# Batch 0 cut into two parts of 384 tokens, in an attention and two-layer kernel on one core

## The chip, the core and the metric

The kernel runs on one core of one Trainium2 chip. The metric is the device time of one execution in microseconds (us); less is better. The time of the kernel before is the median of three runs. A separate execution was recorded by the hardware profiler, and every engine name below is the profiler's: PE is TensorE, DVE is VectorE, ACT is ScalarE, POOL is GpSimd, SP is SyncE, which here only issues DMAs.

## The reference

Attention over 4 batches of 8 heads, 768 positions and 64 elements per head, and a two-layer network with a leaky activation behind it. Three heads (0, 2, 6) see all earlier positions; the other five see the first 4 positions (the sinks) and a window of 64.

```python
scores = scale * np.matmul(q, k.transpose(0, 1, 3, 2))
causal = rel >= 0                              # rel = query position - key position
stream_keep = causal & (is_sink | in_win)      # 4 sinks, window 64
mask = np.where(retr, causal, stream_keep)     # is_retrieval = [1,0,1,0,0,0,1,0]
a = softmax(np.where(mask, scores, -1e9))
x = np.matmul(a, v)                            # to (3072 tokens, 512)
h = x @ w_in                                   # w_in: 512 x 2048
g = np.maximum(h, 0.0) + alpha * np.minimum(h, 0.0)
out = g @ w_out                                # w_out: 2048 x 512, out in float32
```

## The kernel before

**Units of work.** A segment n (0 to 15) is one pair of heads of one batch: batch n // 4, pair n % 4 out of `PAIRS = [(2, 6), (1, 5), (0, 4), (3, 7)]`. So segment 0 holds two full ("retrieval") heads, segments 1 and 3 two windowed ("stream") heads, segment 2 one of each. The keys of a head lie in an array of 128 rows of which 64 belong to that head and the others are zero (`kTs`), so that a score matmul can contract over 128 rows without taking anything from the other head.

**Names in ORDER.** The program is a list of items, `ORDER`, and is issued in exactly that order; each engine works through its own instructions in that order, and so does each DMA queue. An item's name is a letter, a segment, and mostly a head (0 or 1) and a part:

- `Lq`, `Lk`, `Lv` load rows from HBM (issued by SP; a few by ACT and POOL). `Cq`, `Ck`, `Cv` cast them to bf16; for batch 0 to 1 nearly all of these run on POOL. `Cv3.1` is on DVE and includes a copy of the sink rows.
- `Tq`, `Tk` transpose on PE, `tq`, `tk` copy the result out of PSUM. From segment 8 on, `Dq`, `Dk` do this by DMA.
- `S` are score matmuls into PSUM, `s` the exp on ACT that takes them to the buffer of weights (`eR` for full heads, `eS` for stream heads), `m` a multiplication by a 0/1 mask on DVE. Some `m` items (m14.0.2 and its like) cover no masked tile and issue nothing.
- `A` is weights times V on PE, with a column of ones that yields the sum; `a` is its reciprocal and the product on DVE; `X`, `x` transpose the result into `xT`, by PE and a DVE copy, or by a DMA.
- `Pt.f` is the first layer for token part t and block f of 128 hidden columns, four matmuls over the four segments of the batch (for the first blocks of t = 0 split into three items, `P0.f.0` for segments 0 and 1, `.1` for 2, `.2` for 3); `p` is relu(-h) on ACT, `g` the product and sum on DVE. `Ot.s.u` is a quarter of the second layer for 128 tokens, `o` the copy on ACT and the DMA to `out`. `L0` to `L2` and `l0` to `l2` are the last 128 tokens, in three cuts.
- `wi0` to `wi7` and `wo0` to `wo3` load the weights of the two layers through POOL's DMA queue, 256 KB and 512 KB (as bf16). Block f of the first layer needs wi(2k) and wi(2k+1) with k = f // 4. `sz`, `so`, `ro`, `vz`, `kz`, `kfz`, `nz` are fills; `nms`, `nmr`, `ms`, `mr`, `nr`, `ns` make masks.

**Masks and 64-row form.** In batch 0 (n < 4) a mask is added on PE: after each score matmul a second one multiplies the identity with a tile of large negative numbers (lines 466 and 505). From segment 4 on the mask is the item `m`. There, too, score matmuls are collected in a list, `burst`, which is emitted when an item comes up that may not stand beside it (`beside_burst`). If both heads have at least `SPLIT = 576` columns in the list, their matmuls are issued alternately, each on its own 64 rows of the array (line 434), so that two run side by side. Otherwise they are issued one by one over 128 rows (line 427). In batch 0 the scores go out directly (line 417).

**Token parts.** Each batch has two token parts, 512 and 256. A PSUM bank holds 512 columns, so for the 256-token part two blocks f share a bank and one relu. There are eight PSUM banks, taken least recently used first out of a list of choices.

Of the kernel before, what the change touches and what calls it, by code (L numbers as in the profile page):

```python
# [38 lines left out]
O1.0.2 Lk11 s9.0.0 m8.0.3 O1.0.3 x7 P2.4 o1.0 m9.0.0 s8.1.2 S9.1.1 S9.0.1 m8.1.1 m8.1.5 p2.4 S9.1.2 S8.0.5 S9.1.0
m8.0.0 near0 m8.0.1 Lk13 s9.0.2 s8.0.5 s9.1.2 m8.0.4 P2.14 P2.2 s9.1.1 Cv8 s9.0.1 g2.4 m8.1.3 m8.1.4 A8.1 P3.10 P2.3  # L40
p2.2 P2.0 g2.2 Cq10 m8.0.5 a8.1 p2.14 g2.14 p2.0 m9.1.2 P2.1 g2.0 p2.3 P2.7 p2.7 p2.1 A8.0 P3.0 g2.3 P2.5 Ck11 g2.1
P2.9 p2.5 P2.6 g2.7 near2 g2.5 s9.1.0 p3.10 p3.0 p2.9 Cv9 g3.10 P2.8 Lq11 Dk11.1 g2.9 P3.8 m9.1.0 P2.10 p2.8 m9.1.1
Lk12 P3.4 g3.0 A9.1 near1 p2.6 g2.8 Lq13 P2.13 Cq11 P2.15 p2.13 Dk10.1 Dk10.0 Dq10 g2.6 p2.10 g2.13 p3.4 Lq12 P3.6
g2.10 P3.14 p2.15 a9.1 g2.15 P2.11 O2.0.0 P2.12 g3.4 O2.0.1 p2.11 p3.8 g2.11 Ck12 S10.0.1 S10.0.4 s10.0.1 g3.8 p3.14
O2.0.2 s10.0.4 Dk11.0 O2.1.0 Dq11 p2.12 a8.0 g3.14 S10.1.1 S10.0.0 p3.6 g2.12 m10.0.4 S10.1.0 S10.0.5 s10.1.0 s10.1.1
O2.1.1 Lv11 Cq12 O2.0.3 g3.6 S10.0.3 S11.0.0 m10.1.0 s10.0.5 s10.0.0 S11.1.2 S11.1.0 m9.0.2 S10.1.2 S10.0.2 s10.0.3
Cq13 O2.1.2 m10.0.0 s10.1.2 Lv10 Ck13 m9.0.1 m10.1.2 s11.1.2 m11.1.2 s11.1.0 Dk12.0 P3.2 s10.0.2 p3.2 A9.0 s11.0.0
O2.2.0 Dq12 S11.0.2 S11.1.1 m10.0.5 O2.1.3 S11.0.1 m10.0.3 Cv11 m11.0.0 m10.1.1 Dk13.1 m11.1.0 X8 m10.0.1 s11.1.1 Cv10
P3.12 p3.12 m11.1.1 a9.0 s11.0.1 O2.2.1 g3.2 A10.1 Dk13.0 o2.1 Dk12.1 g3.12 a10.1 Dq13 A10.0 A11.1 O2.2.2 m11.0.1 X9
o2.0 O2.3.0 O2.2.3 S12.1.5 S12.0.4 S12.0.2 a10.0 s11.0.2 S12.1.2 m11.0.2 a11.1 S12.0.1 s12.1.5 A11.0 Lq14 a11.0 X11  # L50
# [12 lines left out]
a15.1 A15.0 p5.0 a15.0 p5.4 O4.1.1 g5.8 O4.0.0 a14.0 m4.1.2 O4.2.0 g5.4 X15 P5.10 O4.1.2 O4.0.1 O4.2.1 m8.0.2 x15 X14
O4.0.2 P6.8 P6.6 O4.0.3 p5.10 g5.0 P6.1 O4.3.3 O4.2.2 g5.10 P6.7 p6.8 o4.0 p6.7 p6.6 P7.6 g6.7 g6.8 O4.2.3 P6.10
O4.1.3 P6.3 p6.10 o4.3 g6.10 P7.4 o4.2 O5.1.0 O5.1.1 P7.0 p6.1 g6.6 P6.2 g6.1 p6.3 O5.0.0 g6.3 o4.1 P6.13 p6.13 P7.14
g6.13 O5.0.1 p6.2 p7.0 P6.0 g6.2 O5.1.2 P6.5 g7.0 P6.11 p6.0 g6.0 O5.0.2 p6.11 O5.1.3 p7.4 p6.5 g6.11 P7.10 p7.14
m8.1.2 o5.1 g6.5 m12.1.2 P6.9 P6.4 g7.4 p6.9 g6.9 p6.4 O5.0.3 g7.14 P7.2 O6.1.0 P6.15 g6.4 p7.2 P7.12 p6.15 O6.1.1
O6.1.2 g7.2 o5.0 O6.0.0 g6.15 P6.14 P6.12 O6.0.1 p6.14 O7.0.0 O6.0.2 g6.14 p7.6 p7.12 p6.12 g6.12 g7.6 O6.3.0 O6.2.0
O6.2.1 O6.0.3 P7.8 O6.2.2 O6.1.3 g7.12 O6.3.1 p7.8 o6.1 p7.10 O6.3.2 O6.3.3 g7.8 O7.0.1 o6.3 g7.10 o6.0 L0 O6.2.3
O7.0.2 o6.2 O7.0.3 L1 l0 L2 o7.0 l1 l2  # L70
""".split()


@with_exitstack
def kernel(
    ctx: ExitStack,
    tc: tile.TileContext,
    q: bass.AP,
    k: bass.AP,
    v: bass.AP,  # L80
    is_retrieval: bass.AP,
# [24 lines left out]

    class Tiles:

        def __init__(self, starts, masked):
            self.QS, self.RM = starts, masked  # L110
            self.RO = [sum(S - x for x in starts[:j]) for j in range(6)]
            self.RTOT = sum(S - x for x in starts[:6])
# [13 lines left out]
    def tiles(n):  # L126
        return FULL if full(n) else NEAR if n >= LAY else FAR

# [68 lines left out]
    def heads(n):  # L197
        return PAIRS[n % 4]
# [670 lines left out]
```

## Time and profile before

| what | value |
|---|---|
| runs | 231.18, 230.71, 230.88 us; median 230.88 us |
| profiled execution, span from its first to its last instruction (the profile gives no other time of it) | 230.0 us |
| median of the runs less that span | 0.88 us |
| busy: PE, DVE, ACT, POOL | 221.2, 153.3, 139.1, 47.1 us |
| granted TensorE clock | 1.000 |
| read from and written to HBM | 27.55 MB, 6.29 MB |

Busy time is the time in which an instruction of the engine was in flight. Matmuls are pipelined, so a short matmul counts as long as its latency; the distance between the starts of matmuls that follow each other is a better price. The chain that ended last is followed back from the last instruction, at each step to what released it. The windows cut the span into stretches and give each engine's busy time in them. A row of a group reads: line, engine, operation, output and inputs with shapes, count, busy us and mean ns, then idle time ahead of it and what ended it.

### The profile page before, as it was taken

Reading aid. Unit: us, or ns where it says so; the run is one execution under the profiler, and the core shown is the slowest. Engines: PE = TensorE matmul, PEld = TensorE weight load, DVE = VectorE, ACT = ScalarE, POOL = GpSimd, SP = SyncE. Lnnn points to the kernel's source line nnn. Section 1 sums busy time; section 2 is a strip of 40 time slices with the busy share of each in tenths; the row PEclk is TensorE's granted clock in tenths of the full one; section 3 lists DMA queues with packets and bytes.
Section 4 is the critical chain, followed back from the end, with each engine's and each line's share of the span. In section 5 each row is a group of like instructions: output and inputs, shape, how many; then the busy total and the mean of one; then the engine's idle time right before and its main releaser. Section 6 shows DMA issues by size and latency. Waiting matters only on the chain.

```text
span 230.0 us, 5212 instructions
## 1 busy us (share of the span) xinstructions
PE 221.2 (96%) x1974; PEld 136.7 (59%) x2002; DVE 153.3 (67%) x396; ACT 139.1 (60%) x280; POOL 47.1 (20%) x96
## 2 busy tenths in 40 slices
PE   7989889999999999999999999999999999999994
PEld 7777857555566655565466445556854555554553
DVE  5688768997647866999997349979990345545110
ACT  6679647999968567554864874498422333623232
POOL 6658758000430643000002100010000020000000
PEclk9999999999999999999999999999999999999999
DMA  6979999999999999899979999893310130110033
GB/s 197 299 184 279 246 250 218 231 212 180 209 234 158 230 220 238 157 216 183 184 139 186 211 249 183 163 197 61 62 36 0 48 137 1 46 48 1 0 137 137
DMA packets 92448, 36.62 MB, mean 159 GB/s; under 512 B 79472, under 2 KB 90632, under 8 KB 92424
## 3 DMA queue, kind: packets, MB, share of 16 engines
q1 hardware_dynamic: 86168, 26.97, 59.7%
q0 software_dynamic: 5792, 8.93, 17.3%
q10 hardware_dynamic: 464, 0.40, 0.5%
q8 instruction: 15, 0.25, 0.5%
q14 instruction: 9, 0.07, 0.1%
HBM read 27.55 MB, written 6.29 MB: 147 GB/s over the span
## 4 chain that ended last, share of the span: by engine, by line
PE 85%; DMA 10%; SPq 1%; issue 1%; DVE 1%; POOL 0%; ACT 0%; DVEq 0%
PE P L605 36%; PE P L625 34%; PE P L560 6%; DMA vf<-in_v_dram 5%; DMA kf<-in_k_dram 4%; PE P L434 4%; PE P L644 2%; PE P L427 1%; PE P L585 1%; PE P L369 1%; SPq L247 1%; DVE vb L312 0%; SPq L224 0%; SPq L210 0%; DVE vb L349 0%
## 5 line engine op out<-in xcount | busy, mean ns | idle before, releaser
L617 DVE SCALAR_TENSOR_TENSOR g<-neg,oma,P 128x512 bf16<-128x512 f32 (+1 forms) x128 | 72.9, 610 | 39.7 <-ACT neg L610 38.6
L605 PE MATMUL P<-xT,w_in_b 128*128 128x256 bf16 (+1 forms) x503 | 89.5, 325 | 0.4
L610 ACT ACTIVATE neg<-P 128x512 f32<-128x512 f32 x96 | 54.3, 608 | 52.2 <-PE P L605 43.4
L625 PE MATMUL P<-w_out_b,g 128*128 128x512 bf16 x349 | 84.3, 379 | 1.5 <-issue 0.6
L605 PEld LDWEIGHTS <-w_in_b 128*128 128x128 bf16 x512 | 48.7, 98 | 32.4 <-DVE g L617 0.4
L625 PEld LDWEIGHTS <-g 128*128 128x128 bf16 x368 | 34.5, 98 | 36.8 <-issue 1.3
L473 ACT ACTIVATE eR<-P 128x448 bf16<-128x448 f32 (+6 forms) x63 | 36.6, 621 | 13.6 <-PE P L434 5.1
L635 POOL DMA_DIRECT2D out_dram<-ot x18 | 9.9, 553 | 117.5 <-ACT ot L631 117.5
L571 DVE TENSOR_TENSOR xn<-P,rcp 128x448 bf16<-128x448 f32 (+1 forms) x32 | 19.5, 608 | 1.1
L631 ACT COPY ot<-P 128x512 f32<-128x512 f32 x23 | 13.2, 594 | 11.0 <-PE P L625 8.6
L527 ACT ACTIVATE eS<-P 128x384 bf16<-128x384 f32 (+1 forms) x25 | 13.5, 570 | 3.4 <-PE P L505 2.6
L521 ACT ACTIVATE eS<-P 128x352 bf16<-128x352 f32 x30 | 13.8, 490 | 1.5 <-PE P L427 1.0
L560 PE MATMUL P<-vb,eS 128*128 128x65 bf16 x260 | 11.3, 193 | 1.5 <-DVE vb L312 0.8
L417 PE MATMUL P<-qT,kT 128*128 128x192 bf16 (+13 forms) x68 | 11.5, 251 | 1.1 <-ACT eR L473 0.6
L560 PEld LDWEIGHTS <-eS 128*128 128x128 bf16 x260 | 10.2, 97 | 3.5 <-issue 1.9
L570 DVE RECIPROCAL rcp<-P 128x7 f32<-128x7 f32 (+1 forms) x32 | 6.3, 197 | 7.2 <-PE P L560 6.9
L536 DVE TENSOR_TENSOR eS<-eS,ms_near 128x352 bf16<-128x352 bf16 x30 | 9.4, 336 | 2.3 <-ACT eS L521 2.2
L434 PE MATMUL P<-qT,kT 64*128 64x176 bf16 (+17 forms) x172 | 10.9, 250 | 0.0
L560 PEld LDWEIGHTS <-eR 128*128 128x128 bf16 x276 | 9.6, 97 | 1.5
L434 PEld LDWEIGHTS <-kT 64*128 64x128 bf16 x172 | 6.8, 94 | 6.0 <-issue 5.7
L560 PE MATMUL P<-vb,eR 128*128 128x65 bf16 x276 | 10.1, 193 | 0.0
L483 DVE TENSOR_TENSOR eR<-eR,mr_near 128x128 bf16<-128x128 bf16 (+5 forms) x36 | 6.9, 225 | 4.3 <-ACT eR L473 4.3
(104 smaller groups left out, 183.7 us busy)
## 6 DMA issues: line engine op xcount, KB each, us to landing
out_dram<-ot POOLq DMA_DIRECT2D x18, 256.0 KB, 3.7
vf<-in_v_dram SPq DMA_DIRECT2D x22, 192.0 KB
kf<-in_k_dram SPq DMA_DIRECT2D x21, 192.0 KB
qf<-in_q_dram SPq DMA_DIRECT2D x18, 192.0 KB
qf<-in_q_dram SPq DMA_DIRECT2D x7, 384.0 KB
w_in_b<-in_moe_w_in_dram POOLq DMA_DIRECT2D x8, 256.0 KB, 9.5
w_out_b<-in_moe_w_out_dram POOLq DMA_DIRECT2D x4, 512.0 KB, 13.6
kf<-in_k_dram SPq DMA_DIRECT2D x9, 196.0 KB
```

The costliest lines, as they stand in the source:

```text
L417: nc.tensor.matmul(to, keys, queries, start=True, stop=stop)
L434: nc.tensor.matmul(to, keys[own], queries[own], start=True, stop=True)
L473: nc.scalar.activation(ebuf[n, hh][:, lo:hi].rearrange("p (x c) -> p x c", x=len(parts)), P[:, got[0]:got[0] + len(parts), 0:(hi - lo) // ...
L521: nc.scalar.activation(slots, sc[:, 0:352].rearrange("p (s c) -> p s c", c=176), AF.Exp, scale=scale)
L527: nc.scalar.activation(slots, sc.rearrange("p x (s c) -> p x s c", c=192), AF.Exp, scale=scale)
L560: nc.tensor.matmul(pav[:, i, :], e[:, o:o + 128], vv[:, j, hh, 0:D + 1], start=(m == 0), stop=(m == len(terms) - 1))
L571: nc.vector.tensor_tensor(xn[n][:, 0:nt, D * hh:D * hh + D], pav[:, :, 0:D], rcp.to_broadcast([128, nt, D]), op=ALU.mult)
L605: nc.tensor.matmul(psg[:, w * i:w * (i + 1)], w_in_b[:, c, 128 * fb:128 * (fb + 1)], xT[:, c, o:o + w], start=(x == 0), stop=(x == 3))
L610: nc.scalar.activation(neg[t, f], bank(held["P", t, f][0]), AF.Relu, scale=-1.0)
L617: nc.vector.scalar_tensor_tensor(g_buf[t % 2][:, fb, 0:w], neg[t, f][:, c], oma[:, fb:fb + 1], bank(got[0])[:, c], op0=ALU.mult, op1=ALU.add)
L625: nc.tensor.matmul(bank(held["O", t, s][0]), g_buf[t % 2][:, f, 128 * s:128 * (s + 1)], w_out_b[:, f, :], start=(f == 0), stop=(f == 15))
L631: nc.scalar.copy(ot, bank(got[0]))
```

## The change

Segment 0 is cut at token 384 (`FIRST`): its weights for queries 0 to 383 come first in the buffer, scored as before by `S0.h.0` with masks added on PE; the columns of queries 384 to 767 are four parts `S0.h.1` to `S0.h.4` of 480 columns each, one bank each, handled like those of later batches: collected in `burst`, and masked by `m0.h.3` and `m0.h.4` on DVE. The second exp part of segment 3 (`S3.h.1`) is treated in the same way (`m3.h.1`). `A`, `a`, `X` and `x` of segments 0 and 3 are issued in two parts each (`PARTS`). Batch 0 has token parts of 384 and 384; one block f fills one bank, so both parts have 16 relus of 384 columns. Segment 2's full head and segment 3's heads get weight buffers of their own in the space of `w_out_b`, whose loads come later, and segment 0's result lies in spare space of `g_buf[1]`. The whole of `ORDER` is written anew, from the first load to the last copy.

```diff
-        def __init__(self, starts, masked):
+        def __init__(self, starts, masked, cuts=(S,), ends=None):
             self.QS, self.RM = starts, masked
...
+            self.SEG, self.AT, o = [], {}, 0
+            for lo, hi in zip((0,) + cuts, cuts):
+                for j in range(6):
+                    a = max(lo, starts[j])
+                    if a < hi:
+                        self.SEG.append((j, a, o, hi - a))
...
+    FIRST = Tiles([128 * i for i in range(6)], [128] * 6, (384, S), [0, 384, 768, 1248, 1728, 2208, 2688])
+    PARTS = {0: (0, 3, 6), 3: (0, 4, NT)}
...
+    late = w_out_b.rearrange("p f c -> p (f c)")
+    eR_x = late[:, 0:E_R]
+    eS_x = [late[:, 8192 - E_S * (i + 1):8192 - E_S * i] for i in range(2)]
...
+    ebuf, n_e = {(2, 0): eR_x, (3, 0): eS_x[0], (3, 1): eS_x[1]}, [0, 0]
...
+    def late(n, m):
+        return n >= 4 or n in (0, 3) and m > 0
+
     def score_bank(n, hh, m):
-        held["S", n, hh, m] = got = take(*(SC2 if n < 4 else ANY))
+        held["S", n, hh, m] = got = take(*(ANY if late(n, m) else LOW if n in (1, 2, 3) and m == 1 and not RETR[heads(n)[hh]] else SC2))
...
     def one_score(n, hh, m, to, keys, queries, stop=True):
-        if n < 4:
+        if not late(n, m):
             nc.tensor.matmul(to, keys, queries, start=True, stop=stop)
         else:
             burst.append((n, hh, m, to, keys, queries))
...
-    TOK = [(b * S + o, w) for b in range(B) for o, w in ((0, 512), (512, S - 512))]
+    TOK = [(b * S + o, w) for b in range(B) for o, w in (((0, 512), (512, S - 512)) if b else ((0, 384), (384, S - 384)))]
...
-                if n >= 4:
+                if n >= 4 or n == 0 and m > 2 or n == 3 and m:
                     item(f"m{n}.{hh}.{m}", M_retr if RETR[h] else M_stream, n, hh, m)
```

Of the new ORDER, the stretch from the first V loads to the first layer, and three places where a batch's first layer begins:

```diff
+rox S1.0.0 tq2 s1.0.0 S1.1.1 kfz1 Ck3.0 Ck3.1 Tk3 Lq0.1 S1.0.1 Lv1 Cq0.1 tk2.1 tk2.0 S2.1.0 tk3.0 tk3.1 Tk0.1 s1.1.1
+Cv1 wi1 Lv3 Cv3.0 s2.1.0 S2.1.1 s2.1.1 s1.0.1 tk0.1 S0.0.1 Tq0.1 S0.0.2 Lv0 S2.0.1 s2.0.1 one tq0.1 Cv0 Cv3.1 S3.0.0
+warm1 s3.0.0 s0.0.1 S0.1.0 A3.0.0 S0.1.1 s0.1.0 a3.0.0 s0.0.2 nr A0.0.0 a0.0.0 wi0 S3.1.0 A0.1.0 wi3 szx1 Lv2 Cv2 so1
+s3.1.0 S0.1.2 Lq4 Cq4 A1.1 a0.1.0 Lk5 s0.1.2 wi2 S0.1.3 S3.1.1 s0.1.3 A3.1.0 a1.1 S2.0.0 s3.1.1 s2.0.0 X0.0 sox1
+a3.1.0 wi7 x0.0 S2.0.2 Lk4 X3.0 x3.0 A2.1 a2.1 S3.0.1 s2.0.2 wi6 S0.1.4 s0.1.4 s3.0.1 Tq4 A1.0 Lq5 s0.1.1 m14.0.2
+m0.0.3 A2.0 m0.1.3 a1.0 m0.1.4 A0.0.1 X1 a2.0 A0.1.1 x1 X2 P0.0.0 a0.1.1 x2 P0.2.0 P0.1.0 P0.3.0 P0.3.1 m3.0.1 P0.2.1
+m3.1.1 a0.0.1 Ck5.1 P0.2.2 A3.1.1 tq4 A3.0.1 a3.0.1 P0.3.2 X0.1 P0.0.1 P0.0.2 P0.4.0 P0.1.1 Ck5.0 m12.0.2 Tk5 P0.1.2
...
+S7.0.0 s6.1.0 s7.1.2 Cv6 nz0 A4.1 O0.1.0 O0.1.1 Lv11 s6.0.3 m6.1.1 s7.1.0 s7.0.0 m6.1.0 m7.1.1 a4.1 A6.1 X4 m6.0.3
+m7.0.0 m7.0.2 m7.1.0 m7.1.2 A6.0 X5 A7.0 Lq8 a6.0 a6.1 Cq9 O1.1.2 A7.1 O0.1.2 O1.1.3 X6 a7.0 a7.1 X7 O0.1.3 x6 x5 x7
+P2.1 Lq11 p2.1 g2.1 Ck8 Lv9 Dk9.0 o0.1 P2.14 P3.10 P2.9 p2.9 p3.10 Lq10 P2.15 g3.10 p2.14 g2.14 Dk8.0 P2.12 P2.10
...
+m11.0.2 Dk13.0 m11.0.1 A10.0 a10.0 A10.1 a10.1 O2.0.1 A11.0 a11.0 O3.0.1 O2.0.2 O3.0.2 O3.0.3 O2.0.3 X10 o3.0 X11
+P4.11 o3.1 o2.0 Ck15 P4.9 P5.12 p5.12 p4.9 Lv15 Dq12 P4.5 P4.8 g4.9 p4.5 g4.5 Dk14.1 P4.12 g5.12 Cv13 Lv14 Dq15 p4.12
...
+s14.1.1 s14.1.2 m14.1.2 m14.0.0 m14.1.1 s14.0.2 X12 m14.1.0 A14.1 O5.1.2 a15.0 a15.1 m14.0.3 a14.1 A14.0 O4.1.3 X15
+O5.0.1 O5.0.2 O5.0.3 o5.0 a14.0 X14 x15 P6.1 p6.1 P6.3 p6.3 g6.3 g6.1 o4.1 P6.4 P7.0 p7.0 P7.2 O5.1.3 g7.0 P6.9 p6.4
```

In the order before, the corresponding stretch ahead of the first layer reads:

```
s2.0.2 s3.1.1 ... X1 a2.0 S3.0.1 x1 s3.0.1 kfz1 s3.0.0 Tk4 Cv3.1 wi3 wi6 X2 m6.0.2 Tq5
x2 A3.1 P0.2.0 Lq6 tk4.0 a3.1 A3.0 P0.3.0 Ck5.0 Lq4 tk4.1 a3.0 wi7 P0.0.0 wi5 ms P0.1.0 Al kfz2 X3 Ck5.1 P0.1.1 Tk5
```

## The prediction

> **What bounds the kernel now.** I read the page's busy shares first, then the chain that ended last in order of time, then windows cut where the chain changes its nature. The chain:
>
> ```profile
> PE 85%; DMA 10%; SPq 1%; issue 1%; DVE 1%; POOL 0%; ACT 0%; DVEq 0%
> ```
>
> In order of time it is a start-up led by loads, and from 30 us on TensorE work without a gap:
>
> ```profile
> 20.28 7.32 DMA vf<-in_v_dram
> ...
> 27.69 0.60 DVE vb L349
> ...
> 28.31 1.05 DVE vb L312
> ...
> 29.40 0.50 PE P L560 x11
> ...
> 30.71 1.29 PE P L605 x6
> ```
>
> The last V rows of batch 0 land at 27.69; VectorE casts them and copies the sinks; `A3.1` and the first layer follow. The windows:
>
> ```profile
> core 0: us, PE busy (x) PEld busy (x) DVE busy (x) ACT busy (x) POOL busy (x), PEclk, DMA share, GB/s
> 0.00:29.73 29.73, 25.70 (x384) 22.55 (x385) 22.13 (x57) 21.90 (x29) 20.50 (x44) 1.00 0.99 241
> 29.73:51.32 21.59, 21.43 (x167) 12.97 (x167) 17.97 (x42) 17.07 (x36) 7.39 (x12) 1.00 1.20 227
> ```
>
> Before 29.73 TensorE looks busy, but that is time in flight. To find its work I price matmuls by their spacing in the chain: 216.5 ns for 512 columns (0.86 us for 4), 109 for 256 (0.87 for 8), 56 for 128 (0.34 for 6), 30 for the 65 columns of AV (0.39 for 13); between these 0.421 ns per column. Summed over ORDER: 214.0 us in all, 20.9 ahead of the first P item (`P0.2.0` at 29.73), 193.1 from there. Those 193.1 took until 227.18, 197.45 us: 4.4 us lost in 197, 0.45 of them in the first 3.5 us. So an edit pays in two ways only: an earlier first P item, or fewer columns after it; and it costs by new waits after it. The last output's DMA ends the span 2.8 us after TensorE; the new tail issues the same cuts, so this stays. The profiled span is 230.0, the median of the runs 230.88; I add 0.88 to any span.
>
> **The change, part by part.**
>
> *64-row form.* `emit_burst` interleaves the two heads only if each has 576 columns in the burst. I walked the new ORDER through `beside_burst`: every burst of batch 0 holds one head alone (S0.0.4 | S0.0.3 | S0.0.1 | S0.0.2 | S0.1.1 | S0.1.2 | S0.1.3 with S3.1.1 | S3.0.1 | S0.1.4), because a T, A, non-late S or other item closes each. All fall back to the 128-row form, at the old price. All stand ahead of the first P item too. Gain: 0. (Pairing all would have saved 1920 + 384 columns x 0.421 ns = 0.97 us.)
>
> *Masks to VectorE.* TensorE loses 6 mask matmuls of n = 0 (128 columns, 56 ns) and 6 of n = 3 (192, 148, 44: 82, 64, 30 ns per head): 0.34 + 0.35 = 0.69 us, all in the start-up, where it idles. VectorE gains 6 x 0.225 (the `mr` form of L483 reads 244 ns, its mean 225) + 2 x 0.377 (L534) = 2.1 us.
>
> *Regrouped bursts of later batches:* 10 lone bursts become 7: 0.28 us less.
>
> Sum by the same prices: 213.1 us in all, 20.0 ahead of the first P item (now `P0.0.0`), 193.0 after it. The columns after it are unchanged, so everything turns on when it starts and what is lost behind it.
>
> *384-token parts.* Rows, with the mean ns of one behind the comma:
>
> ```profile
> L610 ACT ACTIVATE neg<-P 128x512 f32<-128x512 f32 x96 | 54.3, 608 | 52.2 <-PE P L605 43.4 <-issue 3.3 <-DVE xn L571 2.6
> L617 DVE SCALAR_TENSOR_TENSOR g<-neg,oma,P 128x512 bf16<-128x512 f32 x64 | 46.5, 744 | 33.1 <-ACT neg L610 32.5
> L617 DVE SCALAR_TENSOR_TENSOR g<-neg,oma,P 128x256 bf16<-128x256 f32 x64 | 27.6, 475 | 6.5 <-ACT neg L610 6.1
> L534 DVE TENSOR_TENSOR eS<-eS,ms 128x384 bf16<-128x384 bf16 x15 | 5.4, 377 | 1.0 <-ACT eS L527 1.0
> ```
>
> Batch 0 has 128 P matmuls as before; 384 columns come to 163 ns, 20.8 us either way. Relu rises from 24 x 0.608 to 32 instructions, each between 0.508 (the 384-column exp of L527) and 0.608; I take 0.508, the nearest shape: +1.7 us on ScalarE. Prelu: 32 of about 0.61 (between 0.475 and 0.744) against 16 x 0.744 + 16 x 0.475: no change. Back to back, an instruction of ScalarE or VectorE starts some 0.12 us before the one ahead has ended (three relus take 1.57 us). At such intervals I count, from `P0.4.0` to `O0.0.0`, ScalarE 15.4 and VectorE 12.9 us beside 17.7 of TensorE: hidden; uncovered the relus would cost 1.7.
>
> *When P0.0.0 can start.* It needs x0.0 and x1, behind a long VectorE queue. Loads of equal cumulated bytes land as before (0.79 MB at 5.5, 1.18 at 7.9, 2.36 at 11.2, 3.15 at 14.3, 4.72 at 21.3, from the casts that waited). VectorE is through tk0.0 and kz1 at 7.7. After that up to x1, at intervals of the trace: 5 split kT copies x 1.13, tk2.0 0.95, tk0.1 0.95, tq0.1 0.93, ms 0.75, some ten fills 1.75, Cv3.1 1.6, four half-size a items x 0.55, four whole ones x 0.77, 6 masks x 0.18, x0.0, x3.0, x1 together 1.1: 20.1 us, so 27.8; the waits that I find by hand (Tk3, A3.0.0) bring 28.4, and 0.5 for handoffs not seen gives 28.9. Bounds: 28.4 without them, 30.5 if VectorE stalls as long as in the same stretch of before (2 us). Gain 29.73 - 28.9 = 0.8, and 0.1 of work.
>
> *Weights of the first layer.* They move behind work on the POOL queue: wi1 behind Cv1; wi0 and wi3 behind Cv0 and `nr` (1.25 us, which ran far behind all weights before); wi2 behind Cv2 and Cq4, which wait for Lv2 and Lq4. Before: issued 18.4 (wi0), 19.9, 23.8, 27.4, and
>
> ```profile
> DMA to landing us min/median/max: 7.1/9.5/11.0
> ```
>
> Now Lv2 lands at 21 to 22.6, so wi2 issues at about 24 to 25.4 and lands between 31 and 35. `P0.4.0` needs it 2.8 us of TensorE work after P0.0.0, at 31.7; all of TensorE queues behind that matmul. Bounds 0 to 3.3 us; I take 0.9, for wi2's own landing before was near 8 us (three pieces' bytes, 0.81 MB, by 32), which gives 32 to 33.4. It replaces the 0.45 lost there before (-0.4). wi0 (about 21.5) lands at 28.6 or later: no margin. [...]
>
> ```profile
> q1 hardware_dynamic: 5548, 3.17, 83.0%
> q0 software_dynamic: 833, 0.81, 34.2%
> ```
>
> (17 to 32 us: weights are q0, 0.81 MB after they begin at 20.) [...] The row alone: 0.81 MB in 12 us is 0.068 MB/us; four pieces are 1.05 MB, 15.5 us from a start near 18.5: 34. That is the slow bound again. SP itself waited until 34.9 for a buffer before (Lq8); now Lq4, Lk5, Lk4, Lq5, Lq7, Lq6 follow without that wait, and keep sharing.
>
> *Layer starts.* P2.1 follows X7 with one O item (0.86 us) as cover for x6, x5, x7; P4.11 follows A11.0 with 4.3 us of O for a11.0 (0.9) and the DMA transposes X10 and X11; P6.1 follows A14.0 with 3.9 for a14.0 and X14. Before, more stood between. X14 alone took 2.5 us from issue (169.56) to its last packet (172.0); under load X10 had 4 to 5. Bounds 0 to 2.5 us over the three; I take 0.6.
>
> *Batch 1's attention packed denser:* S5.1.0 to A4.0 holds 10.4 us of ScalarE beside 10.5 of TensorE (before at most 8.7 beside 9.4): 0 to 1.2, taken 0.4.
>
> Sum: -0.8 - 0.1 - 0.4 + 0.9 + 0.6 + 0.4 = +0.6 on 230.0: 230.6, and with 0.88, **231.5 us**.
>
> **The rivals.**
> *A, the head start holds:* P0.0.0 at 28.4 (-1.3), weights in time, layer starts covered: -1.3 - 0.1 - 0.4 + 0.4 = -1.4, 229.5 us; to 228.6 if ScalarE too keeps pace. For it: all stages but the dense one leave ScalarE a tenth or more. Against: no slack at three places at once.
> *B, weights starve the first layer:* sharing drops q0 below 0.068 MB/us, as from 26 to 28 us (31 packets beside 754); wi2 lands at 35 and wi7, wi6 late for P0.15. It decides once wi2 lands after 31.7, microsecond for microsecond: +3.3 and about 1 behind it in place of 0.9: 234.9 us.
> *C, it doesn't do what it says:* no pairing. That is in my forecast; if pairs form after all, up to 0.97 us comes off TensorE, in a stretch that VectorE's queue covers: 230.5 at best.
>
> **How the numbers follow.** The measurement tells some 0.2% (0.46 us) from no change. Forecast with its own spread (230.4 to 233) 0.52, A 0.31, B 0.12, C 0.05. Faster by over 0.2%: A and a part of C and of the forecast's lower edge, 0.37; same 0.15; slower 0.48. Range 228.8 (A without its outermost) to 234.5 (most of B).
>
> **What would show it.** Right: L434 matmuls at about 180 against 172 (later batches only), lone 128-row ones of the burst at 48 against 32, L505's masks 29 for 35, relu x104; first P matmul near 28.9, with VectorE's xT copy just ahead; a TensorE gap near 32 with w_in as its cause. Wrong: 64-row matmuls before 30 us; the first P item before 28 or after 30.5; P0.4.0 without a gap; TensorE's total loss behind the first P item far from 5.9 us (4.4 + 1.5).

## The result and the profile after

| | before | after |
|---|---|---|
| runs, us | 229.67 to 231.18, median 230.80 | 241.54 to 245.22, median 242.88 |
| ratio | | 1.0521, 95% interval 1.0464 to 1.0579: slower |
| span of the profiled execution | 230.0 us | 243.5 us (the other three: 239.8, 240.7, 241.6) |
| granted TensorE clock, mean | 1.000 | 0.990 |

The sign was the likelier one of the forecast; the size, 12 us, lies far outside the range (228.8 to 234.5). The chain that ended last, which was TensorE and DMA alone, now passes through five kinds of work:

```profile
PE 69%; DVE 10%; DMA 6%; ACT 5%; SPq 5%; issue 3%; POOL 0%; DVEq 0%; ACTq 0%
```

The groups (line, engine, operation, shapes, count, busy us and mean ns, idle before) can be held against the prices of the prediction:

```profile
L646 ACT ACTIVATE neg<-P 128x384 f32<-128x384 f32 x32 | 13.9, 494 | 6.6 <-PE P L639 6.0 <-DVE g L653 0.4
L653 DVE SCALAR_TENSOR_TENSOR g<-neg,oma,P 128x384 bf16<-128x384 f32 x32 | 18.1, 610 | 3.7 <-ACT neg L646 3.4
L558 DVE TENSOR_TENSOR eS<-eS,ms 128x384 bf16<-128x384 bf16 x15 | 6.2, 448 | 5.9 <-ACT eS L551 5.9
...
L458 PE MATMUL P<-qT,kT 64*128 64x176 bf16 (+15 forms) x180 | 11.4, 250 | 0.0
L451 PE MATMUL P<-qT,kT 128*128 128x192 bf16 (+13 forms) x48 | 7.0, 261 | 0.2 <-DVE kT L417 0.2
```

Most are as predicted: relus at 494 ns (taken 508), prelus at 610 (610), 180 matmuls in 64-row form and 48 lone ones, so no burst of batch 0 paired. The stream masks were longer than taken, 448 ns for 377 (batch 0's own two 664). The large difference is not in what is done but in where TensorE stands still. Below, its loss at an item is the time of the item's first matmul less the TensorE work ahead of it, by the prediction's prices. The work is not measured here: it is the prediction's own sum over ORDER, 213.1 us, 1.0 less than before. By it the loss grew from 13.15 to 26.85 us, and the tail behind TensorE's last matmul, read from the traces, by 0.8: -1.0 + 13.7 + 0.8 are the 13.5 us between the spans. The profiled execution of the changed kernel is the longest of its four, so its losses are above those of an execution at the median.

| TensorE's loss, us | up to the first P item | to P2's first | to P4's first | to the end |
|---|---|---|---|---|
| before (from P0.2.0) | 8.8 | 1.9 | 1.6 | 0.9 |
| after (from P0.0.0) | 11.0 | 3.4 | 4.9 | 7.6 |

So 2.2 us were lost at the start, 1.5 in the first layer and batch 1, and 10 from P2 on: in batches 2 and 3, whose attention, layers and masks the change doesn't touch, but whose items it has put in another order. What TensorE waited for (total, times, longest):

```profile
PE P L639 <- DMA xT<-xn: 4.0, 2, 3.1
PE P L589 <- DVE eS L560: 1.7, 1, 1.7
```

Both lie just ahead of batch 2's first layer. The first is `P4.11`, waiting for the DMA transposes `X10` and `X11`. In windows around it (PE busy is the first number behind the length, PEclk the third from the end):

```profile
143.08:146.49 3.41, 0.38 (x1) 0.10 (x1) 0.00 (x0) 0.00 (x0) 0.42 (x1) 1.00 1.02 257
146.49:149.90 3.41, 3.28 (x11) 1.55 (x11) 0.00 (x0) 0.00 (x0) 0.00 (x0) 0.50 1.08 206
149.90:153.31 3.41, 3.36 (x18) 1.69 (x18) 1.82 (x4) 1.93 (x4) 0.00 (x0) 1.00 0.97 206
```

TensorE stood, and when the data came it ran 3.41 us at half clock: 4.3 us of waiting cost 1.7 more. SP's queue (start, length, line, DMA) shows why the transposes came late:

```profile
61.90 2.21 SPq L226 DMA_DIRECT2D qf<-in_q_dram  x2
74.59 0.34 SPq L253 DMA_DIRECT2D vf<-in_v_dram  x1
...
137.11 3.03 SPq L363 DMA_TRANSPOSE kT<-natk  x2
140.24 2.58 SPq L609 DMA_TRANSPOSE xT<-xn  x2
```

From 64.1 to 74.6 `Lv11` stands at the head, waiting for the cast `Cv7`; from 101 to 153 SP issues without a pause, and `X10`, `X11` take their turn at 140.2, though VectorE had finished their data (a11.0) by 138.7. In the kernel before the two were issued at 126.9, a first layer's length ahead of their use. The other wait, `A11.1`, is VectorE's: its queue stood 3.7 us at the cast `Cq15`, whose buffer a transpose of `Dq13` was still reading, with the masks that `A11.1` needed behind it:

```profile
127.38 0.33 DVE L560 TENSOR_TENSOR eS<-eS,ms_near 128x352 bf16<-128x352 bf16 x1
131.41 0.56 DVE L340 CAST natq<-qf 128x768 bf16<-128x768 f32 x1 [3.70 <-DMA qT<-natq]
131.89 0.34 DVE L560 TENSOR_TENSOR eS<-eS,ms_near 128x352 bf16<-128x352 bf16 x1
```

### The profile page after: what moved, and what is told of

It reads as the page before. It is cut to its first block, busy times and chain, and to the rows that moved or that the text cites. A ratio compares the mean times of both kernels' runs of the same rounds, so it can differ in the third digit from the quotient of the medians.

```text
span 243.5 us, 5222 instructions
## 1 busy us (share of the span) xinstructions
PE 226.8 (93%) x1966; PEld 138.7 (57%) x1992; DVE 158.6 (65%) x422; ACT 141.5 (58%) x292; POOL 47.8 (20%) x96
## 4 chain that ended last, share of the span: by engine, by line
PE 69%; DVE 10%; DMA 6%; ACT 5%; SPq 5%; issue 3%; POOL 0%; DVEq 0%; ACTq 0%
PE P L639 28%; PE P L661 25%; PE P L589 5%; PE P L458 3%; DMA kf<-in_k_dram 2%; SPq L363 2%; DMA xT<-xn 2%; PE P L388 2%; DVE eS L558 2%; ACT neg L646 1%; PE P L680 1%; DVE eR L507 1%; DVE g L653 1%; DMA qT<-natq 1%; DVE xn L601 1%
## 5 line engine op out<-in xcount | busy, mean ns | idle before, releaser
L653 DVE SCALAR_TENSOR_TENSOR g<-neg,oma,P 128x256 bf16<-128x256 f32 (+2 forms) x128 | 71.6, 609 | 39.6 <-ACT neg L646 38.7
L639 PE MATMUL P<-xT,w_in_b 128*128 128x512 bf16 (+2 forms) x506 | 88.2, 329 | 5.6 <-DMA xT<-xn 4.0
L646 ACT ACTIVATE neg<-P 128x512 f32<-128x512 f32 (+1 forms) x104 | 55.5, 567 | 49.4 <-PE P L639 38.5
L496 ACT ACTIVATE eR<-P 128x448 bf16<-128x448 f32 (+4 forms) x64 | 34.3, 586 | 5.5 <-PE P L458 2.2
L671 POOL DMA_DIRECT2D out_dram<-ot x18 | 10.2, 568 | 134.2 <-ACT ot L667 134.1
L601 DVE TENSOR_TENSOR xn<-P,rcp 128x448 bf16<-128x448 f32 (+3 forms) x32 | 18.7, 583 | 1.1
L458 PE MATMUL P<-qT,kT 64*128 64x176 bf16 (+15 forms) x180 | 11.4, 250 | 0.0
L551 ACT ACTIVATE eS<-P 128x384 bf16<-128x384 f32 (+1 forms) x21 | 10.5, 565 | 0.8 <-PE P L529 0.5
L558 DVE TENSOR_TENSOR eS<-eS,ms 128x384 bf16<-128x384 bf16 x15 | 6.2, 448 | 5.9 <-ACT eS L551 5.9
L600 DVE RECIPROCAL rcp<-P 128x7 f32<-128x7 f32 (+3 forms) x36 | 6.9, 191 | 3.5 <-PE P L589 1.9
L441 PE MATMUL P<-qT,kT 128*128 128x192 bf16 (+16 forms) x46 | 8.6, 264 | 0.1
## 6 DMA issues: line engine op xcount, KB each, us to landing
w_in_b<-in_moe_w_in_dram POOLq DMA_DIRECT2D x8, 256.0 KB, 10.2
```

The costliest lines, as they stand in the source:

```text
L458: nc.tensor.matmul(to, keys[own], queries[own], start=True, stop=True)
L496: nc.scalar.activation(ebuf[n, hh][:, lo:hi].rearrange("p (x c) -> p x c", x=len(parts)), P[:, got[0]:got[0] + len(parts), 0:(hi - lo) // ...
L551: nc.scalar.activation(slots, sc.rearrange("p x (s c) -> p x s c", c=192), AF.Exp, scale=scale)
L558: nc.vector.tensor_tensor(slots, slots, factor, op=ALU.mult)
L601: nc.vector.tensor_tensor(xn[n][:, i0:i1, D * hh:D * hh + D], pav[:, :, 0:D], rcp.to_broadcast([128, nt, D]), op=ALU.mult)
L639: nc.tensor.matmul(psg[:, w * i:w * (i + 1)], w_in_b[:, c, 128 * fb:128 * (fb + 1)], xT[:, c, o:o + w], start=(x == 0), stop=(x == 3))
```

## The experiments

Theories at the outset: **Q**, SP's pause behind `Lv11` makes everything of batch 2 late; **E/I**, it is the in-order queues of the compute engines; and for the start **V** (VectorE's queue) against **W/S** (loads and weights). All kernels together, each against the kernel before on its own chip. The losses are of the one profiled execution, in the stretches of the table above; its own time stands beside the median, and two rows' losses can be compared only as far as these two agree:

| kernel | median us | profiled, us | ratio to before (95%) | loss: start | to P2 | to P4 | to end |
|---|---|---|---|---|---|---|---|
| changed | 242.9 | 245.2 | 1.052 (1.046 to 1.058) | 11.0 | 3.4 | 4.9 | 7.6 |
| changed, again | 243.4 | 243.9 | 1.055 (1.047 to 1.063) | 12.3 | 2.5 | 4.9 | 6.1 |
| six loads first | 244.0 | 244.4 | 1.054 (1.044 to 1.063) | 12.1 | 3.2 | 3.3 | 7.6 |
| X10, X11 on TensorE | 243.0 | 244.6 | 1.044 (1.032 to 1.055) | 13.6 | 2.6 | 7.3 | 2.1 |
| Cq15 late | 247.6 | 246.7 | 1.076 (1.067 to 1.085) | 10.8 | 4.0 | 3.3 | 10.6 |
| filler matmuls | 243.7 | 243.2 | 1.055 (1.049 to 1.062) | 10.6 | 3.9 | 4.6 | 2.3 (+3.6 filler) |
| the three repairs | 238.7 | 238.7 | 1.037 (1.030 to 1.044) | 11.2 | 4.3 | 1.6 | 2.0 |
| the same, again | 240.7 | 237.8 | 1.041 (1.033 to 1.049) | 10.9 | 3.9 | 1.6 | 2.2 |
| repairs, POOL casts | 241.4 | 239.8 | 1.049 (1.041 to 1.057) | 11.3 | 5.5 | 1.9 | 2.2 |
| before's order for the rest | 253.4 | 254.3 | 1.096 (1.087 to 1.104) | 12.2 | 18.5 | 2.9 | 0.8 |
| before, parts alone | 234.3 | 233.0 | 1.015 (1.009 to 1.022) | 6.6 | 5.0 | 1.6 | 0.8 |
| wi2 early | 244.1 | 249.0 | 1.055 (1.043 to 1.067) | 12.4 | 6.0 | 5.3 | 7.0 |
| wi2 early, masks late | 245.2 | 247.5 | 1.059 (1.048 to 1.069) | 11.4 | 4.0 | 7.0 | 6.9 |
| masks back on TensorE | 245.7 | 249.3 | 1.064 (1.058 to 1.071) | 9.8 | 5.2 | 5.2 | 10.0 |
| repairs + gate | 241.8 | 242.2 | 1.041 (1.031 to 1.052) | 10.5 | 6.4 | 1.8 | 4.2 |
| repairs + gate, masks late | 240.9 | 239.4 | 1.046 (1.037 to 1.055) | 10.9 | 4.9 | 1.6 | 3.0 |
| the same, Q and K later | 241.0 | 242.5 | 1.040 (1.033 to 1.047) | 12.0 | 5.1 | 1.6 | 4.7 |

**Six loads ahead of Lv11.**
```diff
- ... Lq9 m6.1.2 ... Lv11 ... Lq8 ... Lq11 ... Lv9 ... Lq10 ... Lk10 ... Lk11
+ ... Lq9 Lq8 Lq11 Lq10 Lk10 Lk11 Lv9 m6.1.2 ... Lv11
```


> Six loads (Lq8, Lq11, Lq10, Lk10, Lk11, Lv9) go in ORDER from behind Lv11 to right behind Lq9, all else as in the changed kernel (242.9 us, span 243.5). Theory Q (SyncE's queue): Lv11 stands at the head of SP's queue from 64.1 to 74.6 for the cast Cv7, SP issues without a pause from there to 153, and so every later load, cast and transpose of batch 2 is late; the six loads fill that pause with some 8 us of issuing. Then the DMA share between 65 and 80 us rises from 0.36-0.48 to 0.8 or more, X10 and X11 are issued 5 to 8 us earlier, P4.11 waits under 1 us (4.3 now) and the half clock behind that wait goes: 5 to 9 us less, 234 to 238. Theory E (the engines' own order is what is late: casts stand behind ScalarE's and VectorE's work, and a load earlier changes nothing): under 2 us less, 241 to 243, and P4.11 still waits over 3 us.

The pause filled as theory Q said: the DMA share from 65 to 80 us (second to last number) was 0.40 in the changed kernel and is 1.17 here.

```profile
65.00:80.00 15.00, 14.49 (x194) 8.63 (x194) 12.37 (x44) 12.14 (x29) 5.39 (x9) 1.00 1.17 238
```

It brought 1.6 us up to P4 (the pause of 1.4 at P3.0 is gone) and nothing behind it. SP now waited for casts on VectorE instead (5.0 us between 82 and 91, 3.2 before 101.4), joined the old schedule at 101, and came to X10 half a microsecond sooner:

```profile
139.72 2.57 SPq L609 DMA_TRANSPOSE xT<-xn  x2
```

Theory Q as stated falls: the pause was not the root. What holds is its second half, SP's full queue from 101 on.

**X10 and X11 on TensorE.**
```diff
-        elif n >= LAY and n % 4 in XD or n in (4, 11):
+        elif n >= LAY and n % 4 in XD and n != 10 or n == 4:
```


> X10 and X11 become TensorE transposes with a VectorE copy (x10, x11) in place of DMA transposes; nothing else changes. The two DMA transposes are issued at 140.2 to 142.8, behind the two of Dk13 and the loads, and land at 143.1 and 146.6; P4.11 waits 4.3 us for them and TensorE then runs 3.4 us at half clock (1.7 us lost). Theory Q: the wait is the DMAs' place in SP's queue alone, so the wait goes but for the transposes and copies themselves (14 x 0.056 + about 0.6), and the half clock with it: 4 to 6 us less, 237 to 239. Theory E: a10 and a11 are late as well, P4.11 waits on for VectorE: under 2 us less, over 241.

The wait for the DMAs and the half clock behind P4.11 went (loss behind P4: 2.1 for 7.6), but 2.4 us more were lost ahead of it. A11.1 waited 2.2 us in place of 1.7, and this time 3.41 us at half clock followed, which cost 1.7 (PE's wait, and the windows around it):

```profile
PE P L589 <- DVE eS L560: 2.2, 1, 2.2
```

```profile
134.05:137.46 3.41, 1.21 (x20) 0.63 (x20) 3.29 (x15) 0.27 (x1) 0.00 (x0) 1.00 1.42 241
137.46:140.87 3.41, 3.19 (x43) 2.53 (x42) 2.94 (x9) 0.00 (x0) 0.00 (x0) 0.50 0.89 190
```

The new transposes themselves did not wait. So theory Q's wait went as it said, and the time (243.0) was theory E's: VectorE's lateness showed one step earlier, at A11.1. This calls for the two moves by themselves and together.

**Cq15 behind a11.0.**
```diff
- ... s11.1.0 Cq15 m6.0.2 ... A11.0 a11.0 O3.0.1
+ ... s11.1.0 m6.0.2 ... A11.0 a11.0 Cq15 O3.0.1
```


> One item moved: Cq15, the VectorE cast of batch 3's last Q rows, goes in ORDER from between s11.1.0 and m6.0.2 to behind a11.0. In the changed kernel VectorE stood 3.7 us at it (its buffer was still being read by Dq13's transpose), with the masks m10, m11 behind it, and A11.1 waited 1.7 to 2.6 us for those. Theory I (in-order queues: one early item that waits holds up all behind it): A11.1's wait falls under 0.5 us, a10 and a11 come 2 to 3 us earlier, and so do X10 and X11: 2 to 3 us less than the changed kernel on this chip. Theory D (DMA throughput sets that stage, whatever the order): A11.1 no longer waits but P4.11 waits the longer: under 0.7 us less.

A11.1 no longer waited, a11.0 ended 1 us sooner (137.7), and the time rose by 4 us. X10 kept its turn in SP's queue (140.45 against 140.24). TensorE could go on with X10 and X11 at 145.96 and 147.70, in the changed kernel at 143.12 and 146.62, and the DMA share was no higher (1.01 from 141 to 146, there 1.02 from 143.08 to 146.49). Behind the longer pause (4.9 us for 3.1) the clock was at half for 6.83 us in place of 3.41:

```profile
PE P L639 <- DMA xT<-xn: 6.1, 2, 4.9
```

This is theory D's outcome for a reason in SP's queue: here the repair ahead of the last binding wait lengthened that wait (6.1 us for 4.0), and with the second stretch at half clock the time rose by more than the wait grew.

**The three repairs together** (on the chip of the run above, beside the changed kernel again).

> Three repairs at once: the six loads ahead of Lv11 (which alone took the pause at P3.0 of 1.4 us away), X10 and X11 on TensorE, Cq15 behind a11.0. Theory I: the loss behind P2's first item falls from 12.5 to 3 to 5 us, no pause over 1 us and no half clock behind 90 us: 6 to 8 us less than the changed kernel on this chip, 3 to 5 above the kernel before, which is the later start of the first layer. Theory D: at least half of the loss comes back as other waits for DMAs: under 4 us less.

> The changed kernel unaltered, beside the other three on the same chip, so that they can be told against it. Same time as before within its own spread: 241.5 to 244, TensorE losing 12 to 13 us behind P2's first item, with pauses at A11.1 and at P4.11.

238.7 against 243.4 us on the same chip. The losses behind P2 fell from 11.0 to 3.6, and no window from there on lost clock:

```profile
84.00:142.00 58.00, 57.46 (x475) 32.49 (x482) 42.20 (x114) 32.77 (x70) 6.07 (x10) 1.00 1.01 185
142.00:190.00 48.00, 47.59 (x415) 27.79 (x422) 34.42 (x93) 30.37 (x66) 2.15 (x4) 1.00 0.42 90
```

Theory I's losses came as written; in time it was 4.7 us, under the 6 to 8 expected (the two profiled spans differ by 6.0). Alone, the moves had given some 2 us less by its ratio (X10 and X11, within the intervals), nothing (the loads) and 4 us more (Cq15). A second measurement on another chip, as the base of the runs further down, gave 240.7:

> The kernel with the three repairs (238.7 us on the chip before) unaltered, as the base of the two others on this chip: P0.0.0 at 31 to 32.5, P0.4.0 after a pause of 1 to 2.2 us at 35 to 36.5, TensorE's loss behind P2's first item 3.5 us, no half clock.

Behind P2 it lost 3.8 us and no clock, as expected; one half-clock stretch of 3.41 us fell in the start, at 8.2 us.

**Five casts on GpSimd, on top.** `CQ`, `CK`, `CV`: "P" for Cq8, Cq9, Ck8, Ck9, Cv7.

> The same three repairs, and five casts (Cv7, Cq8, Cq9, Ck8, Ck9) on GpSimd in place of VectorE, which is busy 98% from 75 to 80 us and 99% from 100 to 110 while GpSimd is idle four fifths of the span. If VectorE's load is what keeps these casts, and with them SP's transposes, late: another 0.5 to 2 us less than the kernel with the three repairs. If not (GpSimd's casts take 0.8 to 1.2 us for 0.6, and its queue waits for ScalarE at each output): the same within 0.5 us or up to 1.5 us more.

1.1% slower than the repairs, with intervals that still touch: 1.2 us more lost between the first P item and P2 in the profiled execution, with a pause of 1.6 us ahead of A6.0 for a mask on VectorE. That mask, its operands and shape the same, took 0.22 us in the run with the three repairs and 1.47 here, beside two casts on GpSimd from 78.96 to 80.65 (first the run with the repairs, then this one):

```profile
79.15 0.22 DVE L507 TENSOR_TENSOR eR<-eR,mr 128x132 bf16<-128x132 bf16 x1
```

```profile
79.27 1.47 DVE L507 TENSOR_TENSOR eR<-eR,mr 128x132 bf16<-128x132 bf16 x1
```

So the edit took casts off VectorE, and this mask, left there, took 1.25 us longer; whether VectorE's load bound that stretch is not decided by this run.

**Filler in the pause.** 64 matmuls on zeros ahead of P4.11.

> The changed kernel with 64 matmuls of 128 columns on a tile of zeros (3.6 us of TensorE work whose result nobody reads) ahead of P4.11, into the time that TensorE waits for X10 and X11. Seen so far: pauses of TensorE up to 1.69 us left the granted clock at 1.0, those of 1.78 to 3.13 us were followed by 3.41 us at 0.5. If the pause alone takes the clock down: no half clock behind P4.11, P4.9 and P5.12 at full speed, 1.7 us less than the changed kernel though 3.6 us of matmuls were added: 241.2 us. If the clock goes down for another reason: half clock stays, and the time is 242.9 or a little more.

The clock stayed at 1.00 through the stretch, and the wait that was left ended within 0.6 us:

```profile
140.00:150.00 10.00, 9.37 (x95) 6.56 (x95) 1.09 (x2) 3.14 (x6) 1.75 (x3) 1.00 1.04 204
```

The trace shows the effect in the clock alone: 1.00 here, 0.50 in the same place of the changed kernel. The loss behind P4 is 2.3 only because the fillers count as work; with their 3.6 us it is 5.9, beside 6.1 and 7.6. The time, 243.7, is not the 241.2 of this theory but near that of the other (242.9 or a little more): fillers, wait and half clock together come out about even. A gain in time is not shown.

**The later order exchanged.** The changed program with batches 1 to 3 in the order of before, merged by TensorE work.

> The changed program (FIRST, PARTS, masks on VectorE, 384-token parts, buffers) with another ORDER: everything up to 25 us of TensorE work, and all of batch 0 and the first layer, in the changed kernel's order; all that belongs to batches 1 to 3 in the order of the kernel before, merged by the TensorE work done. Theory O (what was lost behind P0.4.0 is lost by the rewritten order of batches 1 to 3: batch 2's loads, casts and transposes come later against TensorE's work, X10 and X11 last of all): TensorE's loss from P2's first item on falls from 12.5 us to 2 to 5, P4's start no longer waits over 1 us, no half clock at P4; 232 to 236 us in place of 242.9. Theory B0 (the loss comes from batch 0's new form itself: first layer without batch 1's attention between, batch 1's attention then denser, ScalarE and SyncE behind from there on): the loss only moves, 239 us or more.

Both were right on a part. From P2's first item on the loss is 3.7 us, with no half clock at P4: as theory O says. But between the first P item and P2 it lost 18.5, so that TensorE came to P2 at 103.6 us and not at 84.2, and the loads of batches 2 and 3 had 19 us more. This run alone therefore can't tell the order from the later start. The three repairs can: they touch batches 2 and 3 alone, reach P2 at 85.3, and brought the loss from there on to 3.6 (the kernel before: 2.5). Why the mixed order loses 18.5 is argued only (batch 1's exps and the first layer's relus then crowd one stretch and its banks). The merge was not tuned, so 253 us says nothing about the best mixed order.

**The kernel before with the 384-token parts alone.** `TOK` and the relu's width as in the change, order of before.

> The kernel before with one part of the change alone: batch 0's tokens in parts of 384 and 384 (32 relus of 384 columns and 16 + 16 prelus in place of 24 relus of 512), each odd P1 item put in ORDER behind the even one's prelu, O0.3's and O0.2's places given to O0.2 and O1.2; attention, masks and all else as before. Theory O: the parts cost nothing, for ScalarE and VectorE keep up with TensorE there: within 0.7 us of the kernel before. Theory B0: the form of the first layer costs of itself: 2 us or more slower than before.

2.0 to 5.1 us slower: theory B0's number, not O's 0 to 0.7. The loss from the first P item to P2 is 5.0 for 1.9, in many stalls of 0.9 us or less. Part of it is the weights, met earlier: the first P item came at 27.5 (29.7 before), and in the longest stall, at P1.6, TensorE waited for w_in.

```profile
PE P L606 <- DMA w_in_b<-in_moe_w_in_dram: 0.6, 1, 0.6
```

So the parts were not free in that order; how much is the 32 shorter relus, how much the weights and how much the places given to the odd P1 items stays open.

**The start.** Four runs turn on P0.0.0 and P0.4.0. In the changed kernel's front (ten profiled executions) P0.0.0 came at 30.6 to 33.6 and P0.4.0 at 35.0 to 36.8, after waits of 0.3 to 2.2 us.

> wi2 moves in ORDER to right behind wi3: it is issued on POOL ahead of Cv2 and Cq4, about 3.5 us earlier (22.9 in place of 26.4). If P0.4.0's gap (0.9 us at 34.1 to 34.95) is wi2's landing, as the prediction had it, P0.4.0 starts 0.7 to 0.9 us earlier and the time falls by that, 242.0 to 242.3. If the gap is ScalarE's (the page names the relu as its releaser), nothing changes: 242.9. If the 256 KB that come earlier push wi0 or wi3 back, P0.0.0 or P0.4.0 starts later than now: 243 to 244.

> wi2 early as in the run before; and the five masks and AVs of batch 0's second part that stand on VectorE and TensorE ahead of X1, x1 and x2 (m0.0.3, m0.1.3, m0.1.4, A0.0.1, A0.1.1 and a0.1.1) go behind x2, with banks 6 and 7 for them. Theory V (the start is VectorE's queue: it works from 18.6 to 32 with 0.45 us of pauses): x1 ends 1.3 us earlier, P0.0.0 starts at 29.7 (31.05 now), P0.4.0 at 32.5 to 33: 1.5 to 2.2 us less, 240.7 to 241.4. Theory W (loads and weights bind the start): P0.0.0 stays at 30.5 or later, or P0.4.0 waits up to 34 again: under 0.9 us less.

> The changed kernel with one part undone: the masks of batch 0 are added on TensorE again (12 matmuls, +0.69 us of TensorE work) and VectorE's eight multiplications (2.1 us by the prediction) are left out; order, parts and buffers as changed. Theory V (VectorE's queue sets the start: x1 ends as P0.0.0 begins, 31.06 and 31.05): 1.4 us of these masks stand ahead of x1, P0.0.0 starts 1 to 1.5 us earlier, P0.4.0 then waits the longer for wi2 (34.95 stays or 34.5 at best): the time changes by 0 to -0.5 us. Theory W (loads set the start): P0.0.0 does not move, or later by the matmuls: 0 to +0.7 us.

wi2, issued at 23.8 and 23.0 us in place of 26.3, did not land sooner (37.2 and 35.4; 34.8 in the changed kernel): issue to landing of a w_in piece (last number, median us) went from 10.2 to 12.9, and P0.4.0 waited 2.2 us.

```profile
w_in_b<-in_moe_w_in_dram POOLq DMA_DIRECT2D x8, 256.0 KB, 12.9
```

With the masks out of VectorE's queue P0.0.0 came at 30.6 (masks late) and 30.5 (masks on TensorE), at the early edge of the ten, and P0.4.0 still at 35.5 and 36.3. Neither gained time, and that VectorE bounds P0.0.0 is seen in one trace (x1 ends as P0.0.0 begins) but not shown by these runs. P0.4.0 is held by wi2: in each of the ten and in all three of these runs it began 0.1 to 0.2 us after wi2 had landed (34.98 after 34.8 in the changed kernel). From 22 to 27 us of the changed kernel (packets, MB, share of the DMA engines) the weights' queue q0 has a quarter of them:

```profile
q1 hardware_dynamic: 1497, 1.31, 83.1%
q0 software_dynamic: 235, 0.23, 28.2%
```

So SP's queue was held until x0.0:

```diff
+    item("Lg", nc.sync.dma_start, gate, moe_alpha.rearrange("(a p) -> a p", p=128)[:, 0:64])
+    fill("gm", gate, 0.0)       # in ORDER: ... wi3 wi2 ... x0.0 gm Lg Lk5 Lk4 Lq4 Lq5 ...
```

> On the base of the three repairs: SP's queue is held until x0.0 (about 26 us) by a DMA of 4 KB into a tile that VectorE clears just behind x0.0; the loads Lk5, Lk4, Lq4, Lq5 and all behind come after it (22 to 31 us before), wi2 is issued right behind wi3, and the items that need those loads (Cq4, Tq4, tq4, Tk5) go some 3 to 6 us later in ORDER. Theory S (the weights of the first layer are late because loads take the DMA engines: 1.31 MB of loads beside 0.23 MB of weights from 22 to 27 us): the four pieces land by 30, P0.4.0 waits under 0.4 us: 1.5 to 2 us less than the base, unless batch 1's later loads cost it again. Theory P (wi2's place on POOL, or the weights' own rate): P0.4.0 waits over 1 us as before and the time stays within 0.5 us or rises.

> The same, and the masks and AVs of batch 0's second part behind x2 (as in the run with wi2 early and masks late, with the two AVs one P item later). Theory V: x1 comes 1.3 us earlier, P0.0.0 at 29.7 to 31 on this chip; with the weights in time the time falls by another 0.8 to 1.3 us: 2.3 to 3.3 less than the base. If weights or loads still bind, nothing more than in the run with the gate alone.

> As the run with gate and masks late, but Tq4, tq4 and Tk4 stand behind P0.7, four P items (2.6 us of TensorE work) later in ORDER. Theory S with a debt that can be paid late: no pause at Tq4, P2.1 reached 1.3 to 2 us earlier than in that run (84 in place of 85.6), 2 us less than it: 0.8 to 1.2% under the base of the three repairs. If batch 1's attention then waits for Q and K instead (debt only moved): a pause near the first S4 and S5 items, and the same time within 0.7 us.

Theory S is shown: with the loads held, q0 has the engines in that stretch, a piece lands in 6.6 us (median), wi2 lands at 30.2, and P0.4.0 starts without a wait at 32.9.

```profile
q0 software_dynamic: 550, 0.53, 71.3%
q1 hardware_dynamic: 273, 0.07, 6.1%
```

And the gain, 2.5 us at P0.4.0, was given back 3 us later and more: TensorE waited for the cast of the load that had been held, 3.41 us at half clock followed (1.7 us), and P2 came at 86.8, where the base has 84.6 and 85.3 in its two traces:

```profile
PE P L389 <- POOL natq L341: 2.0, 1, 2.0
```

Four P items more of distance took this pause away, and stalls came at P1.1 (0.9 us) and at P4.10 (1.6); P2 came at 87.0. None of the three is faster than the repairs alone. Loads and weights together keep the DMA engines busy 0.9 or more from 6 to 55 us in the changed kernel, and in these three runs, with wi2 sooner, P2 came at 86.8, 85.6 and 87.0.

## Why the prediction was wrong, and where it was right

**Layer starts (+0.6, bounds 0 to 2.5): the step that failed.** It was sized from `X14`, alone on a quiet queue, 2.5 us from issue to last packet, and it took the cover to be the O items between A11.0 and P4.11 (4.3 us). What decided was SP's turn: X10 and X11 were issued at 140.2, behind two K transposes, though X10's data were ready at 138.0 and X11's at 138.7, and they took up to 5.0 us to land beside V loads and K transposes (DMA share 1.0). P4.11 lost 4.3 us and the half clock behind it 1.7, together 6.0, against 0.6 for three places. The prediction did not walk SP's queue in batch 2.

**A term that wasn't there.** The sum had nothing for batches 2 and 3 between the layer starts. P3.0 lost 1.4 us (Lk10 late) and A11.1 2.1 (Cq15). The prediction argued that "the columns after it are unchanged"; the order of the loads and casts behind those columns was not, and the three repairs, which change nothing ahead of batch 2, bring the loss from P2 on back from 11.0 to 3.6 (the kernel before: 2.5): some 7 to 9 of the 10 us.

**The start (-0.8): wrong sign.** P0.0.0 came at 31.05. The working counted 20.1 us of VectorE from 7.7; it was 21.0 from 8.0, and the waits were 2.1, where 1.1 was taken. The prediction's own upper end, waits as long as in before, would have given 30.5.

**wi2 at P0.4.0 (+0.9): right cause, and a size that was luck.** The wait was 0.9 us in the profiled execution, 0.3 to 2.2 in nine others, but wi2 landed at 34.8, rival B's 35 and not the 32 to 33.4 that was taken. The wait came out at 0.9 only because P0.0.0 itself was 2.1 us late; P0.4.0 began at 34.98, 2.4 us behind the 32.6 that the sum implied. The bytes argument (0.068 MB/us for the weights) held better than the issue times: issued sooner, wi2 landed no sooner (37.2 and 35.4 for 34.8); with the loads held, it did (30.2). From issue to landing of a w_in piece the medians of the runs go from 6.6 to 12.9 us.

**Batch 1 denser (+0.4) and the parts hidden (0).** Between P0.4.0 and P2.1 the changed kernel lost 2.2 us, as much as the kernel before between its first P item and P2 (1.9), and mostly some 0.2 us at each paired burst, as there: the term was small, as said. That the parts are hidden held in the new order, and not in the order of before.

**Right:** no burst of batch 0 pairs (180 matmuls in 64-row form, 48 lone ones); the prices of relu and prelu. **Wrong as a whole:** the total loss behind the first P item, 15.9 us where 5.9 was the mark that it had set. The span came 12.9 us above the forecast's 230.6: 2.1 from the start, 10.0 from those losses (P4.11 with its half clock 5.4 above its term, P3.0 1.4, A11.1 2.1, small ones 1.1), and 0.8 from the tail, which was said to stay at 2.8 us and was 3.6. The tail is 3.3 to 3.7 in all kernels that end in the new order and 2.8 to 2.9 in the three that end in the old; its cause is open. In rival A, 228.6 is the span ahead of the 0.88: by its own terms the time was 229.5 less 0.4, 229.1.

## What to carry to other kernels

A change that comes with a new order is priced on every in-order queue it passes, DMA issuing ones first, and through to the end of the program, not up to the last changed item: here 10 of the 13.7 us of new losses arose in batches that compute what they did before. Waits in a row did not add up here, so find the one that binds last and mend it first or all at once: mending an earlier one alone (Cq15) made the last one longer (6.1 us for 4.0). And moving loads out of the way of weights, or the reverse, was no gain here, where the DMA engines were 0.9 busy or more: look at bytes, then at issue times.

## What the hardware showed unexpectedly

By these traces the granted clock changes on a grid of 3.41 us: within each run the starts of half-clock stretches lie whole numbers of 3.413 us apart (28, 33, 42, 64 of them), and each lasts 3.41 or 6.83 us. What went with the change is TensorE's busy time in the window of this grid just ahead. In the eighteen traces, from 3 us behind the first matmul on, 16 windows at full clock had it busy for 0 to 0.44 of their length; 15 of them were followed by half clock (the other is one of 0.44 in the kernel with the later order exchanged). Of the windows at full clock above 0.45 only one was (0.52, in the same trace). Behind a window that was itself at half clock it differs: busy 0.56 (Cq15 late) and 0.71 (masks back on TensorE) were followed by a second one, which are the 6.83 us. Two windows at full clock, busy for 0.40 and 0.46 of their length, each with the one behind it (length, then PE busy; PEclk third from the end):

```profile
21.41:24.82 3.41, 1.36 (x22) 1.19 (x22) 3.31 (x5) 0.86 (x2) 3.41 (x5) 1.00 0.90 198
24.82:28.23 3.41, 3.41 (x37) 2.88 (x36) 2.31 (x10) 2.43 (x5) 2.06 (x5) 0.50 1.08 311
```

```profile
131.80:135.21 3.41, 1.56 (x18) 0.74 (x17) 3.37 (x14) 0.89 (x3) 0.00 (x0) 1.00 1.36 246
135.21:138.62 3.41, 3.36 (x65) 2.40 (x63) 3.15 (x12) 0.00 (x0) 0.00 (x0) 1.00 1.09 193
```

The first pair is the kernel with X10 and X11 on TensorE, a pause of 1.78 us; the second the changed kernel again, a pause of 1.79 us that fell in a window with a little more work. So one pause of 1.8 us cost 1.7 us more and another nothing, and this can be one source of the 2 to 3 us by which runs of one kernel differed; it is not the only one, for the lowest mean clock of the changed kernel's four (0.979) is not that of its longest. The expectation of the filler run had put it down to the pause's length alone; pauses of 2.1 us (the changed kernel again) and 2.8 us (masks back on TensorE), lying across the edge between two such windows, kept full clock.
